# A tuned attention-and-feed-forward kernel: the order of its five queues is read from a table, and 185 operations go to VectorE

## The chip, the cores and the metric

The kernel runs on one core of one Trainium2 chip. The metric is device time in microseconds (us) of one execution, the median of the runs shown. A core has five instruction queues that matter here: TensorE (PE; its weight loads are listed apart as PEld), VectorE (DVE), ScalarE (ACT), GpSimd (POOL) and SyncE (SP), which in this kernel only issues DMAs. Each queue runs its own instructions in order, and the queues meet through semaphores.

## The reference

```python
def phi(x):                                   # q and k scaled by D ** -0.25
    h = x @ omega.T - sum(x * x, -1) / 2
    return exp(h - max(h, -1)) / sqrt(M)
kv, z = phi(k)^T @ v, sum(phi(k), tokens)     # one batch and head at a time
x = phi(q) @ kv / (phi(q) @ z + 1e-6)         # heads laid side by side: 4608 x 512
out = leaky_relu(x @ w_in, 0.01) @ w_out      # 512 -> 2048 -> 512
```

Eight batches of 576 tokens, eight heads of 64, 128 random features; everything in and out is float32.

## The kernel before, in words

**The work.** Attention goes batch by batch over the keys (`key_batch`) and in nine blocks of 512 tokens over the queries (`query_block`), two heads at a time. A float32 operand is written as two float16 parts (`high` copies the upper part, L479 on ACT or its twin L473 on DVE; `low_` subtracts to get the lower one, L485, on POOL or DVE), and a product is three float16 matmuls. For one unit of two heads (class `Unit`) the chain is: load (`nat`, L719), square on ACT (L722), sum on DVE (L724), scales (L729 to L734), split (L479 and L747 or L485), DMA transpose `t<-z` (L749), projection on PE (L762), maximum and subtraction on DVE (L770 to L790), exponential on ACT (L793), split again (L479, L485), and for queries two DMA transposes `qp<-ph` (L1060) and the product with the key sums on PE (L1092 to L1094). A finished block is turned by DMA into `xt` (L1029). The first two key batches and the first query block take a shorter way (class `Whole`, L846, L975, L1099).

**The feed-forward part.** For each block of 512 tokens PE runs a first layer (L1254 for blocks 0 and 1; L1308 from block 2 on, in a form that needs seven products in place of eight, whose weights `w<-w1d` are loaded for each product, L1298) and a second (L1490; L1415 for the last block, `TAIL`). These two are TensorE's filler between the attention pieces. One operation of the plan on PE is 6 matmuls of 512 columns or 12 of 256. Results leave PSUM by ACT or DVE (L479, L1324, L1263, L1331) and are split into `big` (L479, L485).

**The order.** Nothing is ordered by hand. Each operation is registered with `ways` (engine, modelled cost, function to call). `Plan.forward` (L195) lays all operations on five modelled queues one after another; for an operation with two ways it takes the engine that looks free first, weighted by `PRICE`. Its list is the program's order: `for o in plan.order(): o.run()` (L1548). The numbers of operations are the order in which the kernel registers them, so a number means the same operation before and after. Heat operations (L569) are matmuls without use that the planner puts into gaps of PE near the start. Constants steer the planner: `PACE`, `AFTER`, `SLACK`, `NUDGE`, `LATER`, `PRICE`, and the modelled landing of a DMA, `DMA`. 701 operations have a choice of engine; before, 700 of them are on ACT (548) or POOL (152) and one is on DVE.

Of the kernel before, what the change touches and what calls it, by code (L numbers as in the profile page):

```python
# [30 lines left out]
SIGN_POOL = {"w1": [0, 1, 2, 4, 5, 7], "w2": [0, 1, 3, 7]}  # L31
SPLIT_DVE = {"w1": [0, 1, 2, 4, 5, 7], "w2": [0, 1, 2, 3, 4, 5, 6]}
Z_POOL = {"k": 4, "q": 3}
PACE = {"k": 17.0506, "q": 9.3419, "w1": 0, "w1s": 4.2874, "w2": 12.4675, "w2s": 14.7789}

WHOLE = 2
FIRST_FAST = 2
TURNED = 1
HEAT = True
AFTER = {"w1": 0.0, "w1s": 0.0, "w2": 0.0, "w2s": 0.0, "k1": 0.0, "q1": 0}  # L40
PASSES = 0
SHIFT_OP = {180: -1.13, 6: -3.99, 178: 2.07, 213: -0.22, 420: 3.05, 572: -0.02, 480: -0.72, 242: -1.74, 250: -2.72, 106: -1.06, 268: -4.94, 148: -4.28, 85: -4.22, 813: 0.8, 510: 2.03, 109: 2.11, 452: 11.66, 574: 2.34, 243: -2.55, 245: -6.52, 430: 4.22, 69: 19.05, 135: 1.83, 476: -3.51, 209: -10.73, 167: 1.07, 75: -11.31, 536: -3.21, 54: 2.69, 203: -3.67, 218: -23.73, 152: 1.07, 137: -0.51, 238: -0.14, 168: 2.42, 811: 24.59, 116: -2.3, 454: -3.25, 518: -0.29, 44: 0.47, 494: -5.44, 239: -5.28, 580: 6.23, 191: -6.7, 855: 8.61, 275: -6.71, 236: 4.8}
WHOLE_ACT = ['k10']
EDGE_ACT = ['k02', 'k03']
SQ_POOL = ['k02', 'k13', 'q02']
LOW_ACT = {"w1": [3], "w2": [1, 4, 5]}
FFN_MI = [2, 2]
TAIL = 7
ROWS_LATE = 4
TAIL_ON = {"A11": ["DVE"], "A22": ["DVE"], "S1": ["POOL"], "S3": ["POOL"], "S2": ["DVE"], "A12": ["DVE"], "S4": ["POOL"], "T1": ["DVE"], "T2": ["DVE"], "T3": ["POOL"], "T4": ["DVE"]}  # L50
TAIL_DOWN = 2.0 ** -2
OPS = ("A11", "A12", "A22", "S1", "S2", "S3", "S4")
SLOT = {"B11": 0, "B21": 1, "B22": 2, "B12": 3, "T1": 4, "T3": 5, "T2": 6, "T4": 7}
SLACK = {"PE": 0.5, "t": 0.5608, "qp": 0, "ph": 0.6854, "mx": 0, "w": 0.2511, "chain": 0}
# [30 lines left out]

class Op:
# [3 lines left out]
class Plan:  # L90
# [21 lines left out]
    def op(self, ways, r=(), w=(), prio=0.0, slack=0.0, moved=0):  # L112
# [235 lines left out]
def act(n, pointers=0):  # L348
    return 0.17 + n / 1195 + 0.06 * pointers
# [19 lines left out]
def performer_ffn(ctx: ExitStack, tc, qT, kT, qn, kn, vn, omT, eye, w_in, w_out, out):  # L369
# [143 lines left out]
    def power_of_two(mx, name, prio, one_=ONE):  # L513
# [60 lines left out]
    class Weight:  # L574
# [27 lines left out]
        def convert(self, i, prio):  # L602
# [22 lines left out]
            def sums():  # L625
# [76 lines left out]
    class Unit:  # L702
# [49 lines left out]
        def features(self, c0, nc_, ph, part):  # L752
# [54 lines left out]
    class Whole:  # L807
# [5 lines left out]
        def __init__(self, what, i, hp, prio):  # L813
# [20 lines left out]
        def features(self, c0, nt, p32, p):  # L834
# [5 lines left out]
            def project():  # L840
# [101 lines left out]
    def key_batch(b, prio):  # L942

        plan.group = f"v{b}"
        plan.after = AFTER["k1"] if b == 1 else 0.0
        values(b, prio)
# [4 lines left out]
        for hp in range(HP):  # L951
            plan.like("k", PACE["k"])
            plan.after = AFTER["k1"] if b == 1 else 0.0
            plan.group = f"k{b}{hp}"
# [13 lines left out]
            if b < WHOLE:  # L968
                def sums(u=u, edge=edge, acc=acc, hp=hp, parts=parts):
# [232 lines left out]
    def tail_weights():  # L1202

        for q in range(4):
# [20 lines left out]
            for name, i in (("T3", 2), ("T2", 1), ("T1", 0), ("T4", 3)):  # L1225
# [3 lines left out]
                low_(512, lambda part=part: part(1), lambda t=t, i=i: t(i), lambda part=part: part(0),  # L1229
                     engines=TAIL_ON[name], r=[key(i), (tt, 0)], w=[(tt, 1)], prio=LATER["t"])  # L1230

    def feed_forward(j):
# [38 lines left out]
        def split(name, q, g):  # L1271
# [325 lines left out]
```

## Time and profile before

| | us |
|---|---|
| median of 3 runs | 926.81 (924.36 to 930.95) |
| the profiled execution's own time | 923.68 |
| its span, first to last instruction | 921.9 |
| PE busy in the span | 892.6 (97%) |
| DVE busy | 734.2 (80%) |
| ACT busy | 604.0 (66%) |
| POOL busy | 347.5 (38%) |
| DMA, share of 16 engines, mean | 74% |

Busy is the time in which an engine has at least one instruction under way. Matmuls overlap and their ends are modelled, so a PE that is busy 97% of the time is read together with its list of waits. The span is 1.8 us under the execution's own time.

### The profile page before, as it was taken

The page shows a single profiled execution, that of the slowest core. Times are in us where ns is not written, and L with a number is a line of the kernel's source. Part 1 is how long each engine was busy: PE and PEld are TensorE (multiplying, and loading weights), DVE is VectorE, ACT ScalarE, POOL GpSimd, SP SyncE. Part 2 cuts the span into 40 slices and gives each one's busy share as a digit, 9 for nine tenths or more (in the row PEclk, how much of TensorE's full clock was granted, in tenths as well). Part 3 has the DMA queues.
Part 4 walks back from the last instruction along what each step waited for, and adds up shares of the span by engine and source line. Part 5 has one row for each costly group of instructions (what it writes and reads, how often), then busy time and mean ns, then how long its engine had stood idle before and what let it go on. Part 6 is the DMA issues. An engine that isn't in the chain of part 4 may idle for free.

```text
span 921.9 us, 20740 instructions
## 1 busy us (share of the span) xinstructions
PE 892.6 (97%) x8247; PEld 641.4 (70%) x8247; DVE 734.2 (80%) x1390; ACT 604.0 (66%) x945; POOL 347.5 (38%) x297
## 2 busy tenths in 40 slices
PE   7999999999989999999999989999999999999998
PEld 6887554555547875687558855785579656888887
DVE  6998988887878989777787888889789789862751
ACT  6787896577655975388558864796568645842741
POOL 2422567579532560136013611261124622330330
PEclk9999999999999999999999999999999999999999
DMA  9976547855599998989689988897679963733401
GB/s 352 366 241 183 116 107 190 187 111 124 125 255 240 279 226 182 198 231 227 155 174 249 249 178 197 208 259 170 153 191 259 199 137 113 198 75 94 135 2 47
DMA packets 274881, 170.14 MB, mean 185 GB/s; under 512 B 191072, under 2 KB 237920, under 8 KB 273760
## 3 DMA queue, kind: packets, MB, share of 16 engines
q1 hardware_dynamic: 274784, 168.82, 73.9%
q8 instruction: 64, 1.05, 0.5%
q14 instruction: 33, 0.27, 0.1%
HBM read 105.87 MB, written 16.78 MB: 133 GB/s over the span
## 4 chain that ended last, share of the span: by engine, by line
PE 67%; DVE 14%; DMA 9%; ACT 5%; issue 3%; SPq 2%; POOL 1%; DVEq 0%; ACTq 0%; POOLq 0%
PE ffn L1490 11%; PE late L1490 10%; PE late L1308 10%; PE ffn L1308 9%; DMA t<-z 6%; PE late L1415 5%; PE ffn L1254 4%; PE pj L762 4%; PE late L1254 4%; PE ffn L1415 3%; DMA qp<-ph 2%; PE mi L975 2%; DVE ph L485 1%; DVE st L770 1%; DVE p L790 1%
## 5 line engine op out<-in xcount | busy, mean ns | idle before, releaser
L1308 PEld LDWEIGHTS <-w 128*128 128x128 f16 x2352 | 228.4, 98 | 34.8 <-issue 5.1
L485 POOL TENSOR_TENSOR big<-row,big 128x512 f16<-128x512 f32 x118 | 155.6, 1331 | 199.8 <-ACT big L479 183.7
L1490 PEld LDWEIGHTS <-big 128*128 128x128 f16 x1344 | 128.5, 98 | 140.6
L1490 PE MATMUL ffn<-wt,big 128*128 128x512 f16 x672 | 156.3, 379 | 0.0
L1490 PE MATMUL late<-wt,big 128*128 128x512 f16 x672 | 156.1, 379 | 0.0
L1308 PE MATMUL late<-xt,w 128*128 128x256 f16 x864 | 118.0, 273 | 0.7 <-ACT nat L479 0.7
L1308 PE MATMUL ffn<-xt,w 128*128 128x256 f16 x840 | 115.6, 273 | 1.0 <-ACT row L479 1.0
L793 ACT ACTIVATE p<-p,little 128x1024 f32<-128x1024 f32 (+1 forms) x60 | 61.0, 1017 | 65.5 <-DVE p L790 61.2
L770 DVE TENSOR_REDUCE st<-pj 128x8 f32<-128x1024 f32 x68 | 73.3, 1077 | 26.0 <-PE pj L762 25.9
L479 ACT ACTIVATE big<-row 128x512 f16<-128x512 f32 x130 | 78.8, 625 | 4.1 <-DVE row L1280 3.4
L485 DVE TENSOR_TENSOR ph<-p,ph 128x1024 f16<-128x1024 f32 x56 | 72.5, 1294 | 5.6 <-ACT ph L479 5.6
L762 PEld LDWEIGHTS <-t 128*128 128x128 f16 x944 | 57.2, 98 | 16.4 <-DMA t<-z 5.8
L762 PE MATMUL pj<-om,t 128*128 128x128 f16 x944 | 63.9, 219 | 4.1 <-DMA t<-z 2.7
L790 DVE SCALAR_TENSOR_TENSOR p<-pj,sc,st 128x1024 f32<-128x1024 f32 (+1 forms) x60 | 67.1, 1118 | 0.9
L724 DVE TENSOR_REDUCE sq<-z 128x8 f32<-128x512 f32 (+1 forms) x56 | 39.6, 708 | 32.9 <-ACT z L722 32.6
L1254 PEld LDWEIGHTS <-w 128*128 128x128 f16 x384 | 36.7, 98 | 40.4
L722 ACT ACTIVATE z<-nat 128x512 f32<-128x512 f32 (+1 forms) x56 | 36.4, 653 | 35.7 <-DMA t<-z 31.9
L479 ACT ACTIVATE ph<-p 128x1024 f16<-128x1024 f32 x56 | 59.1, 1055 | 0.9
L1308 PE MATMUL late<-w,w 128*128 128x256 f16 x324 | 53.0, 272 | 2.1 <-ACT row L479 2.1
L485 POOL TENSOR_TENSOR xn<-xp,xn 128x768 f16<-128x768 f32 (+1 forms) x16 | 27.7, 1733 | 69.0 <-ACT xn L479 68.2
L1308 PE MATMUL ffn<-w,w 128*128 128x256 f16 x324 | 53.0, 273 | 0.0
L1331 ACT ACTIVATE row<-row 128x512 f32<-128x512 f32 x72 | 44.5, 625 | 7.8 <-DVE row L1324 7.6
(272 smaller groups left out, 1847.3 us busy)
## 6 DMA issues: line engine op xcount, KB each, us to landing
w<-w1d SPq DMA_DIRECT2D x196, 256.0 KB, 3.4
v<-vn SPq DMA_DIRECT2D x28, 650.0 KB, 4.8
big<-w_in SPq DMA_DIRECT2D x8, 1024.0 KB, 11.7
big<-w_out SPq DMA_DIRECT2D x8, 1024.0 KB, 5.9
nat<-qn SPq DMA_DIRECT2D x32, 256.0 KB, 3.6
out<-row SPq DMA_DIRECT2D x29, 256.0 KB, 2.5
w1d<-wt SPq DMA_DIRECT2D x16, 256.0 KB, 3.1
nat<-kn SPq DMA_DIRECT2D x12, 320.0 KB, 4.2
```

The costliest lines, as they stand in the source:

```text
L479: ("ACT", act(n, int(pointer)), lambda: nc.scalar.activation(dst(), src(), AF.Copy, scale=1.0 if scale is None else value()), False),
L485: return ways([(e, c, lambda g=g: g.tensor_tensor(dst(), a(), b(), op=ALU.subtract), True) for e, c, g in (("POOL", pool_(n), nc.gpsimd), ...
L724: op("DVE", dve(n), lambda: nc.vector.tensor_reduce(at(self.sq)[:, :2 * nt], square().rearrange("p (g d) -> p g d", d=D), axis=AX.X, op=AL ...
L762: nc.tensor.matmul(at(pj)[:, 512 * h + c * M:512 * h + (c + 1) * M], at(self.t)[:, 2 * (c0 + c) + h, :], om[:, w, :], start=(w == 0), stop ...
L770: op("DVE", dve(n * M), lambda: nc.vector.tensor_reduce(row(0), pv(), axis=AX.X, op=ALU.max), r=[pj], w=[st], prio=prio)
L790: op("DVE", dve(n * M), lambda: nc.vector.scalar_tensor_tensor(p(), pv(), down(), row(2).rearrange("p (g o) -> p g o", o=1).broadcast_to([ ...
L793: op("ACT", act(n * M, 1), lambda: nc.scalar.activation(flat(p()), flat(p()), AF.Exp, bias=shift), w=[p32], r=["ones"], prio=prio)
L1254: nc.tensor.matmul(at(ph), wk[wp][:, c:c + P], xt[:, 512 * xp:512 * xp + 512], start=(i == 0), stop=(i == 3 * KT - 1))
L1308: nc.tensor.matmul(pair(bank)[:, f], wt[:, k, wp, f * P:f * P + P], operand(xname, k, xp), start=(first and f == k == i == 0), stop=(k == ...
L1331: op("ACT", act(512), lambda: nc.scalar.activation(at(g), at(src), AF.Prelu, scale=H_DOWN * (TAIL_DOWN if tail else 1.0), alpha=0.01), r=[ ...
L1415: nc.tensor.matmul(pair(bank)[:, t], g()[:, gp, f, t * P:t * P + P], operand(wname, 2 * q + f, wp), start=(first and q == t == f == i == 0 ...
L1490: nc.tensor.matmul(at(po), g_(q)[:, s, gp, t * P:(t + 1) * P], wf[wp], start=(q == s == 0 and gp == wp), stop=(q == s == 3 and gp == 1))
```

## The change

`Plan.order` still calls the planner, with other constants, and buffers get their places from it. Then, since the table `ORDER` is not empty, 185 operations listed in `ON` are set to DVE and the planner's list is replaced by the table's. The tiles, the loops, the buffers' numbers and the arithmetic are the same.

```diff
-AFTER = {"w1": 0.0, "w1s": 0.0, "w2": 0.0, "w2s": 0.0, "k1": 0.0, "q1": 0}
+AFTER = {"w1": 0.0, "w1s": 0, "w2": 0, "w2s": 0.0, "k1": 13.2731, "q1": 0}
-SQ_POOL = ['k02', 'k13', 'q02']
-LOW_ACT = {"w1": [3], "w2": [1, 4, 5]}
+SQ_POOL = ['k13', 'q02']
+LOW_ACT = {"w1": [0, 3], "w2": [1, 2, 4, 5]}
-TAIL_ON = {"A11": ["DVE"], ... "T3": ["POOL"], "T4": ["DVE"]}
+TAIL_ON = {"A11": ["POOL"], ... "T3": ["DVE"], "T4": ["DVE"]}
-DMA = {"turn": 0.9497, "land": 1.9}
+DMA = {"turn": 0.959, "land": 1.9}
-PRICE = {"PE": 1.0, "ACT": 0.5, "DVE": 27.4627, "POOL": 1.0, "SP": 1.0}
+PRICE = {"PE": 1.0, "ACT": 0, "DVE": 27.4627, "POOL": 1.0804, "SP": 1.0}
...
+ORDER = [
+    2, 0, 16, 1, 144, 151, 27, 3, 165, 43, 17, 4, 62, 22, 9, 5, 7, 18, 6, 145, 23, 146, 152, 3478, 19, 81, 3461, 158,
...
+    2092, 1879, 1869, 1894, 2300, 1880, 2091, 1886, 2340, 2071, 2319, 2289, 1887, 2288, 2075, 2361, 2301, 2128, 2072,
+    1888, 2341, 2302, 2342, 1895, 2343, 2303, 2306, 2093, 2320, 2304, 1912, 2094, 2290, 1902, 2151, 2307, 2658, 2076,
...
+]
+ON = {
+    102: "DVE", 282: "DVE", 309: "DVE", 310: "DVE", 340: "DVE", 360: "DVE", 365: "DVE", 369: "DVE", 375: "DVE",
...
+}
...
             done = self.forward()
+        if ORDER:
+            by = {o.number: o for o in done}
+            assert len(by) == len(ORDER)
+            for n, e in ON.items():
+                o = by[n]
+                o.engine, (o.cost, o.run, o.held) = e, o.ways[e]
+            done = [by[n] for n in ORDER]
         return done
```

`PACE`, `SLACK`, `NUDGE` and `LATER` change too. Read operation by operation, with the numbers of the kernel before:

- **Engines.** Of the 185 operations in `ON`, 131 were on ACT and 54 on POOL. The POOL ones are 41 splits of `big`, 11 of `xn`, 2 of `wt` (all L485). Of the ACT ones 98 copy from SBUF (55 of them a `row` into `big` or its last-block twin `g7`, 512 elements each) and 33 from PSUM. 154 of the 185 stand between 80 and 800 us of the trace before, 30 behind 800, one before 80.
- **Order.** PE's operations keep 168 of 768 places; the mean shift is 1.8 places and the largest 14. The mean shift is 2.3 places on ACT, 3.1 on DVE, 1.1 on POOL and 4.6 on SP.
- **Distance between a DMA and its first user**, counted as the PE work that the list has between the two (1.31 us for a PE operation of the feed-forward part, by its duration in the trace):

| DMA | list before, median | table, median | under 4 us, before / table | under 5.2 us, before / table |
|---|---|---|---|---|
| `qp<-ph`, L1060, 64 | 5.5 | 6.5 | 20 / 2 | 28 / 10 |
| `t<-z`, L749, 56 | 5.3 | 6.5 | 7 / 4 | 18 / 13 |
| `w<-w1d`, L1298, 196 | 17.8 | 14.9 | 0 / 3 | 0 / 8 |

Inside a run of seven products (L1308), an operation that adds to a bank after ScalarE has copied it out stands 1.31 us of PE work or more behind the operation that filled the bank before, and 2.6 us or more in the table. The shortest distance of a weight load is 11.8 us before; in the table the eight shortest are 3.6, 3.9, 3.9, 4.3, 4.4, 4.8, 4.8 and 4.8 us. As an example, transpose 2092 (`qp<-ph`) and its user 2093 have the PE operations 1887, 1895, 1888 between them before (3.9 us) and 1894, 1886, 1887, 1888, 1895, 2306 in the table (6.7 us).

- **Start.** Ahead of the first feed-forward operation (296, L1254) the list before has 54 operations of PE and 89 of DVE; the table has 56 and 91. The 1024 KB load of the first weight piece (144) is issued as the fourth DMA that moves data, before as the seventh.

## Rows read from the trace of the kernel before

**Rows 1.** Windows: us, then each engine's busy time, clock, DMA share, GB/s
```profile
0.00:80.00 80.00, 69.14 (x798) 63.14 (x799) 69.63 (x123) 58.73 (x80) 25.95 (x20) 0.98 0.86 308
80.00:800.00 720.00, 705.59 (x6373) 472.88 (x6373) 608.07 (x1185) 494.08 (x770) 294.71 (x257) 1.00 0.81 189
800.00:922.00 122.00, 117.88 (x1080) 105.41 (x1078) 56.54 (x83) 51.18 (x97) 26.81 (x21) 0.99 0.27 77
```

**Rows 2.** Waits of PE, 80 to 800 us: total us, times, longest
```profile
PE mi L1094 <- DMA qp<-ph: 6.0, 7, 2.1
PE pj L762 <- DMA t<-z: 2.7, 5, 1.3
PE late L1308 <- ACT row L479: 2.1, 2, 1.4
PE pj L762 <- DVE p L790: 1.4, 3, 0.6
PE ffn L1308 <- ACT row L479: 1.0, 2, 0.7
PE late L1308 <- ACT nat L479: 0.7, 1, 0.7
PE mi L1092 <- DMA qp<-ph: 0.3, 1, 0.3
```

**Rows 3.** Timeline of PE: start us, us, what, idle before and its releaser
```profile
546.41 0.20 PE L1093 MATMUL mi<-kv,qp 128*128 128x65 f16 x1
548.68 0.20 PE L1094 MATMUL mi<-kv,qp 128*128 128x65 f16 x1 [2.08 <-DMA qp<-ph]
```

**Rows 4.** Line L1060, the transposes of queries
```profile
L1060 SPq DMA_TRANSPOSE qp<-ph x64: 1231/1252/3188, 116.0 to 754.6; - x64
...
DMA to landing us min/median/max: 3.0/3.5/7.3
```

**Rows 5.** Line L749, the transposes ahead of the projection
```profile
L749 SPq DMA_TRANSPOSE t<-z x56: 1231/1304/2842, 99.3 to 738.2; - x56
...
DMA to landing us min/median/max: 3.0/4.0/7.4
```

**Rows 6.** Line L1298, the weight loads of the first layer
```profile
DMA to landing us min/median/max: 2.5/3.4/6.4
```

**Rows 7.** Groups: line, engine, tiles, count; busy us, mean ns; idle before
```profile
L485 POOL TENSOR_TENSOR big<-row,big 128x512 f16<-128x512 f32 x118 | 155.6, 1331 | 199.8 <-ACT big L479 183.7 <-PE ffn L1308 14.5 <-DVE st L780 1.3
L479 ACT ACTIVATE big<-row 128x512 f16<-128x512 f32 x130 | 78.8, 625 | 4.1 <-DVE row L1280 3.4
L1324 DVE TENSOR_TENSOR row<-ffn,row 128x512 f32<-128x512 f32 x40 | 27.3, 685 | 8.9 <-ACT row L479 4.6 <-PE ffn L1308 4.1
L780 DVE SCALAR_TENSOR_TENSOR st<-st,sc,sq 128x8 f32<-128x8 f32 (+1 forms) x60 | 23.6, 393 | 0.3
```

**Rows 8.** Single lines on DVE: ns min/median/max, first and last start
```profile
L485 DVE TENSOR_TENSOR big<-row,big x12: 679/692/1282, 795.6 to 890.5; 128x512 f16<-128x512 f32 x12
```

**Rows 9.** The same for L619, a DVE operation with one SBUF input
```profile
L619 DVE TENSOR_SCALAR wt<-wt x12: 680/683/1593, 11.7 to 103.3; 128x1024 uint32<-128x1024 uint32 x12
```

**Rows 10.** The same for L780, an 8-element DVE operation with SBUF inputs
```profile
L780 DVE SCALAR_TENSOR_TENSOR st<-st,sc,sq x60: 191/220/1349, 109.1 to 746.7; 128x8 f32<-128x8 f32 x48, 128x2 f32<-128x2 f32 x12
```

**Rows 11.** Timeline of DVE, 235 to 239 us
```profile
236.36 1.22 DVE L485 TENSOR_TENSOR z<-nat,z 128x512 f16<-128x512 f32 x1
237.50 1.12 DVE L780 SCALAR_TENSOR_TENSOR st<-st,sc,sq 128x8 f32<-128x8 f32 x1
238.65 2.06 DVE L781 SCALAR_TENSOR_TENSOR st<-sq,st 128x8 f32<-128x8 f32 x1
```

**Rows 12.** Timeline of POOL in the same stretch
```profile
237.41 1.19 POOL L485 TENSOR_TENSOR big<-row,big 128x512 f16<-128x512 f32 x1 [0.38 <-ACT big L479]
238.56 2.13 POOL L485 TENSOR_TENSOR wt<-wt,wt 128x1024 f16<-128x1024 f32 x1
```

**Rows 13.** Chain that ended last, in order of time: start, us, what
```profile
410.75 1.31 PE late L1308 x12
```

More of the change, by code (lines that the diff above doesn't have):

```diff
@@ L33 @@
 Z_POOL = {"k": 4, "q": 3}
-PACE = {"k": 17.0506, "q": 9.3419, "w1": 0, "w1s": 4.2874, "w2": 12.4675, "w2s": 14.7789}
+PACE = {"k": 17.0506, "q": 9.3419, "w1": 0, "w1s": 4.0808, "w2": 12.256, "w2s": 14.7789}
 WHOLE = 2
@@ L49 @@
 ROWS_LATE = 4
-TAIL_ON = {"A11": ["DVE"], "A22": ["DVE"], "S1": ["POOL"], "S3": ["POOL"], "S2": ["DVE"], "A12": ["DVE"], "S4": ["POOL"], "T1": ["DVE"], "T2": ["DVE"], "T3": ["POOL"], "T4": ["DVE"]}
+TAIL_ON = {"A11": ["POOL"], "A22": ["DVE"], "S1": ["POOL"], "S3": ["POOL"], "S2": ["DVE"], "A12": ["DVE"], "S4": ["POOL"], "T1": ["DVE"], "T2": ["DVE"], "T3": ["DVE"], "T4": ["DVE"]}
 TAIL_DOWN = 2.0 ** -2
@@ L53 @@
 SLOT = {"B11": 0, "B21": 1, "B22": 2, "B12": 3, "T1": 4, "T3": 5, "T2": 6, "T4": 7}
-SLACK = {"PE": 0.5, "t": 0.5608, "qp": 0, "ph": 0.6854, "mx": 0, "w": 0.2511, "chain": 0}
-NUDGE = {"k00": -25.85, "w24": 1.48, "q61": -21.35, "k10": 1.26, "k51": 12.31, "q00": -3.82, "k53": 5.68, "w20": -28.23, "w2s6": 9.28, "k12": -43.23, "w1s0": 20.35, "q41": 14.5, "w1s4": -31.95, "w2s5": 11.73, "q72": -10.0, "q03": -13.54, "w1s7": 11.67, "w2s7": 35.19, "k61": -6.69, "w13": -6.9, "w2s3": -4.27, "q10": 7.76, "s1": 15.36, "k50": -31.99, "q70": 16.75, "q02": -0.99, "q40": 0.78, "k42": 7.0, "w25": 5.84, "q63": -12.37, "w27": 17.73, "k11": -8.86, "w26": -23.6, "w2s2": -6.21, "v0": 2.9, "s4": 26.82, "k20": -6.57, "w2s1": -14.47, "q13": 74.22, "w2s4": 0.58, "s5": -0.19, "k02": -14.86, "q32": -6.67, "k62": -10.59, "w14": -8.71, "q11": -1.54, "q01": -26.27, "q62": 19.06, "w1s1": 23.47, "q22": -11.17, "v1": 56.53, "q20": -2.28, "w21": 0.21, "q81": -4.21, "k32": -5.66, "w22": 5.41, "q42": -23.84, "w16": 25.18, "q80": 26.73, "k01": -35.93, "v7": -21.02, "q83": 11.84, "s0": -8.64, "k71": 9.99, "q71": -17.15, "w2s0": -2.21, "w23": 2.17, "w1": 3.97, "q60": 18.36, "q53": -3.85, "v4": 9.32}
@@ L56 @@
-DMA = {"turn": 0.9497, "land": 1.9}
+SLACK = {"PE": 0.5, "t": 0.5608, "qp": 0, "ph": 0.7205, "mx": 0.3817, "w": 0.2686, "chain": 0}
+NUDGE = {"k00": -34.58, "w24": 0.31, "q61": -21.35, "k10": 1.26, "k51": 18.64, "q00": -9.35, "k53": 5.68, "w20": -27.85, "w2s6": 11.07, "k12": -43.23, "w1s0": 20.05, "q41": 14.5, "w1s4": -34.51, "w2s5": 11.73, "q72": -10.0, "q03": -13.54, "w1s7": 3.85, "w2s7": 35.19, "k61": -6.69, "w13": -6.72, "w2s3": -4.27, "q10": 7.76, "s1": 15.36, "k50": -31.99, "q70": 16.75, "q02": -0.99, "q40": 0.78, "k42": 7.0, "w25": 5.84, "q63": -12.37, "w27": 14.68, "k11": -8.86, "w26": -75.24, "w2s2": 14.2, "v0": 2.9, "s4": 26.82, "k20": -6.57, "w2s1": -14.47, "q13": 78.87, "w2s4": 25.02, "s5": -18.23, "k02": -14.86, "q32": -3.42, "k62": -7.66, "w14": -30.08, "q11": -1.54, "q01": -26.27, "q62": 19.06, "w1s1": 23.47, "q22": -11.17, "v1": 47.01, "q20": -2.28, "w21": 21.39, "q81": -4.21, "k32": -5.66, "w22": 19.42, "q42": -23.84, "w16": 25.18, "q80": 26.73, "k01": -35.93, "v7": -28.3, "q83": 11.84, "s0": -8.64, "k71": 18.32, "q71": -17.15, "w2s0": -2.21, "w23": -4.68, "w1": 3.97, "q60": 18.36, "q53": -3.28, "v4": 10.69, "w11": -66.92, "q73": 5.16, "k33": -16.25, "w1s3": 13.51, "w1s2": -13.38, "q23": -12.35, "k03": -0.78, "w12": 12.32, "s6": 10.1, "q12": 3.31, "k31": 5.31, "w15": 2.14, "w2": -2.65, "k70": -10.63, "s7": -2.01}
@@ L60 @@
 SUMS_DVE = [2, 6]
-LATER = {"w1": -37.7982, "w2": 48.514, "k": -26.2825, "q": -902.8399, "t": 0.05, "f": 0.0319, "s": -0.0449}
+LATER = {"w1": -37.7982, "w2": 48.514, "k": -17.5267, "q": -866.6901, "t": 0.0594, "f": 0.0319, "s": -0.0696}
 ONE = 2.0 ** 14
@@ L83, in __init__ @@
         self.kind, self.place, self.ops, self.left, self.last = kind, None, [], 0, None
+ORDER = [
[172 rows of a table added]
+]
+ON = {
+    102: "DVE", 282: "DVE", 309: "DVE", 310: "DVE", 340: "DVE", 360: "DVE", 365: "DVE", 369: "DVE", 375: "DVE",
+    415: "DVE", 483: "DVE", 534: "DVE", 561: "DVE", 596: "DVE", 607: "DVE", 632: "DVE", 667: "DVE", 685: "DVE",
+    690: "DVE", 695: "DVE", 700: "DVE", 704: "DVE", 705: "DVE", 715: "DVE", 720: "DVE", 725: "DVE", 730: "DVE",
+    735: "DVE", 745: "DVE", 813: "DVE", 828: "DVE", 851: "DVE", 861: "DVE", 908: "DVE", 953: "DVE", 956: "DVE",
+    963: "DVE", 1040: "DVE", 1088: "DVE", 1096: "DVE", 1104: "DVE", 1134: "DVE", 1140: "DVE", 1170: "DVE",
+    1203: "DVE", 1259: "DVE", 1278: "DVE", 1281: "DVE", 1288: "DVE", 1297: "DVE", 1316: "DVE", 1322: "DVE",
+    1365: "DVE", 1366: "DVE", 1373: "DVE", 1378: "DVE", 1390: "DVE", 1391: "DVE", 1398: "DVE", 1399: "DVE",
+    1404: "DVE", 1411: "DVE", 1419: "DVE", 1422: "DVE", 1430: "DVE", 1443: "DVE", 1462: "DVE", 1468: "DVE",
+    1508: "DVE", 1528: "DVE", 1538: "DVE", 1590: "DVE", 1600: "DVE", 1651: "DVE", 1688: "DVE", 1695: "DVE",
+    1704: "DVE", 1712: "DVE", 1748: "DVE", 1787: "DVE", 1792: "DVE", 1804: "DVE", 1813: "DVE", 1819: "DVE",
+    1850: "DVE", 1865: "DVE", 1868: "DVE", 1874: "DVE", 1910: "DVE", 1982: "DVE", 2004: "DVE", 2026: "DVE",
+    2034: "DVE", 2041: "DVE", 2052: "DVE", 2118: "DVE", 2127: "DVE", 2140: "DVE", 2141: "DVE", 2146: "DVE",
+    2147: "DVE", 2158: "DVE", 2173: "DVE", 2178: "DVE", 2179: "DVE", 2191: "DVE", 2198: "DVE", 2199: "DVE",
+    2205: "DVE", 2227: "DVE", 2244: "DVE", 2274: "DVE", 2372: "DVE", 2385: "DVE", 2409: "DVE", 2416: "DVE",
+    2434: "DVE", 2440: "DVE", 2471: "DVE", 2483: "DVE", 2496: "DVE", 2497: "DVE", 2528: "DVE", 2529: "DVE",
+    2532: "DVE", 2537: "DVE", 2540: "DVE", 2541: "DVE", 2549: "DVE", 2554: "DVE", 2572: "DVE", 2581: "DVE",
+    2604: "DVE", 2609: "DVE", 2610: "DVE", 2615: "DVE", 2616: "DVE", 2704: "DVE", 2740: "DVE", 2753: "DVE",
+    2777: "DVE", 2788: "DVE", 2838: "DVE", 2841: "DVE", 2855: "DVE", 2905: "DVE", 2926: "DVE", 2935: "DVE",
+    2980: "DVE", 2995: "DVE", 3002: "DVE", 3025: "DVE", 3031: "DVE", 3040: "DVE", 3049: "DVE", 3052: "DVE",
+    3061: "DVE", 3064: "DVE", 3080: "DVE", 3100: "DVE", 3162: "DVE", 3165: "DVE", 3166: "DVE", 3216: "DVE",
+    3219: "DVE", 3240: "DVE", 3244: "DVE", 3249: "DVE", 3252: "DVE", 3267: "DVE", 3282: "DVE", 3286: "DVE",
+    3294: "DVE", 3309: "DVE", 3312: "DVE", 3321: "DVE", 3333: "DVE", 3336: "DVE", 3339: "DVE", 3345: "DVE",
+    3363: "DVE", 3378: "DVE", 3394: "DVE", 3414: "DVE", 3415: "DVE",
+}
```

169 rows, old and new, of the table ORDER are left out of this document.

## The prediction, made before the changed kernel ran

> **What bounds the kernel now.** I read the windows first, then the waits of TensorE (PE), then single lines. In the windows [rows 1] the reader is to see three stretches. From 80 to 800 us PE is busy 705.59 of 720 us, so 14.4 us are idle. In the first 80 us it idles 10.9 us while VectorE (DVE) is busy 69.63 of 80, its densest stretch (87%): the start is paced by DVE. Behind 800 us PE is busy 117.88 of 122 us and the other engines are under half busy; the rest is mostly the end, when the last result is stored. So PE is the bound, its arithmetic is untouched, and only its idle time can be won.
>
> The waits between 80 and 800 us [rows 2] sum to 14.2 us: 9.0 us for transposes (6.0 + 2.7 + 0.3, 13 waits), 3.8 us for ScalarE (ACT) copying a bank out (2.1 + 1.0 + 0.7, five waits), 1.4 us for DVE. One of them shows what such a wait is: PE had begun a product, and its second half of `qp` came 2.08 us late [rows 3].
>
> **The change, part by part.**
>
> *Transposes issued farther ahead.* A `qp` transpose lands 3.0 us after its issue at best, 3.5 in the median and 7.3 at worst [rows 4]; `t` takes 3.0, 4.0 and 7.4 [rows 5]. The list before has 27 of the 120 less than 4 us of PE work ahead of their user; the table has 6. Nearly every late one is moved by one PE operation, 1.31 us [rows 13]; the one of rows 3 goes from 3.9 to 6.7 us, more than its wait. The gain lies between 0 (the issue itself slips, since a transpose leaves only when its split is done) and 9.0 us. I scale the wait by the count of short distances, 6 of 27, which leaves 2.0 us: **-7.0 us**. I lean to this end because the longest wait, 2.1 us, is under two operations.
>
> *Bank copies.* Each of the five waits for ACT is at most 1.4 us, and the table puts one more operation of 1.31 us between such a pair. Between 0 and -3.8 us; I take **-3.0 us**, since ACT also gets shorter: 131 operations at about 0.63 us [rows 7] leave it, some 82 of its 604 us. The 1.4 us that wait for DVE I leave as they are.
>
> *Weight loads issued later.* This is what the table pays with. Eight of 196 loads now stand less than 5.2 us ahead of their product and three less than 4 us, against 11.8 us or more before; they land in 2.5 us at best, 3.4 in the median, 6.4 at worst [rows 6]. At the median nothing is late. If all eight landed at the worst time (distances 3.6, 3.9, 3.9, 4.3, 4.4, 4.8, 4.8, 4.8 us) they would cost 2.8 + 2.5 + 2.5 + 2.1 + 2.0 + 3 x 1.6 = 16.7 us. So 0 to +16.7; nearest to the median, **+1.0 us**.
>
> *185 operations to DVE.* Their price there:
> - 54 from GpSimd (POOL), 32256 elements per partition. The same split on DVE takes 692 ns for 512 [rows 8], against 1331 ns on POOL [rows 7]: 43.6 us.
> - 33 from PSUM, at 685 ns for 512 [rows 7]: 20.2 us.
> - 98 copies from SBUF, 58112 elements. DVE does no such copy in the trace. Nearest is L619, one SBUF input, 683 ns for 1024 [rows 9]: 38.8 us. The other end is the two-input split's pace, 692 for 512: 78.5 us. I take the lower, since L619 has the same number of inputs.
>
> Of this 88.7 us (low) or 121.3 us (high) fall between 80 and 800, where DVE has 608.07 us busy and 112 us idle [rows 1]. Neighbours on DVE overlap by 0.08 us (236.36 + 1.22 against 237.50) [rows 11], so 154 more instructions give back 12 us. That makes 685 us (95%) or 717 us (99.6%), before what POOL's lighter load gives back. L780 works on 8 elements in 220 ns but took up to 1349 [rows 10]: it started at 237.50 beside a POOL split of 237.41 to 238.60 and ended with it, and the next, at 238.65, lasted as long as POOL's 2.13 us [rows 11, 12]. So DVE loses time to POOL, and POOL loses 54 operations, about 81 of its 347 us. L780's waits alone are 60 x (393 - 220) ns by its mean [rows 7], 10 us; I put the whole relief at 5 to 20 us by that one line, and nothing of it in the sum. What covers the added DVE work is the distances above; if that cover is gone, each step of a unit's chain passes its delay to the next transpose. Cost at the low price: **0**, at the high price the rival below.
>
> The Trainium skill, "SBUF — State Buffer", section "Who interferes with whom", speaks against part of this: VectorE and GpSimd share a port pair, a copy in a two-port mode takes it for its whole length, "PE and ACT never wait on anyone". The trace agrees on the lock (220 to 1349 ns, above). By that rule the 98 copies, free of waits on ACT, enter the contention; the sum would then lose the relief and nothing more, since the 54 splits leave it.
>
> *Smaller edits.* Two weight conversions get their first step on ACT in place of DVE, one square goes from POOL to ACT, four splits of the last block go from DVE to POOL and four the other way. All have free time beside them in the first or last stretch: 0, at most 1 us either way.
>
> *Start and end.* PE's and DVE's work ahead of the first feed-forward operation grows by two operations each, at most +3 us; the first weight piece is loaded earlier, into a DVE that idles 10 us, at most -5 us. I take 0. The end keeps its order of stores: 0.
>
> *Queues passed.* SP issues in order and waits in order. A transpose that moves ahead is moved past plain loads; a load that waits for its ring place then holds the transposes behind it. That is inside the bounds of the first and third part.
>
> **Sum**: -7.0 - 3.0 + 1.0 = -9.0 us on the profiled execution's 923.7, so 914.7. The median of the runs stands 3.1 us above that execution, which was the lowest. What separates the runs is not shown; I keep a little of it and forecast **915 us**.
>
> **The rivals.**
> - *DVE takes over what the DMAs gave.* The transposes are issued late because their splits are: DVE at 95% runs each unit's chain later by about what the table gained. For: DVE is the fullest engine off the bound, and the operation at 238.65 shows how late a small step on it can be [rows 11]. Against: POOL's relief. Gain of the first part gone, ACT's kept: 923.7 - 3 + 1 = 922, with the median's excess **924 us**.
> - *Weight loads late (slower).* Place: the runs of products between 290 and 875 us. Price: 16.7 us, and the transposes queued behind gain nothing: 923.7 + 16.7 - 3.0 = 937. It decides from the point at which these loads land later than 4.4 us on the average. **937 us.** Against: the median of 3.4.
> - *DVE at the high price (slower).* At 99.6% with no relief it must run without any idle time; its densest stretch reached 87%. If 95% is the most it can do, 717 us need 755: **about 958 us**. Against: L619's pace.
> - *More than the sum.* All 14.2 us of waits go and the start gives 4: **905 us**.
> - *The table does not say what I read*: the chip's order would be the same but for the engines; then about 926 us. The replay is plain in the diff, so this is small.
>
> **How the numbers follow.** About 1% (9.3 us) is what a measurement of this kernel can tell from no change. Chances: forecast 0.55 (its own range 909 to 921, two thirds of it under 917.5), DVE takes over 0.20, more than the sum 0.12, weight loads 0.07, DVE at the high price 0.04, the rest 0.02. Faster: 0.37 + 0.12 + 0.02 = 0.51; same: 0.18 + 0.18 + 0.02 = 0.38; slower 0.11. The range goes from 904 to 930: below it lies little of the fourth case, above it the two slow ones.
>
> **What would show it.** Right: PE's waits for `qp` and `t` between 80 and 800 us fall from 9.0 to about 2 us, those for ACT from 3.8 to under 1, PE idle there from 14.4 to some 6 us; DVE's busy time in that stretch rises to between 660 and 700 us and L780's mean falls from 393 ns. Wrong: a new wait of PE for `w<-w1d`; copies on DVE at 0.6 us or more for 512 elements; waits for DVE above 5 us; or a start whose first feed-forward matmul comes more than 3 us later than before.

## The result and the profile after

| us | before | after |
|---|---|---|
| median | 925.59 (923.56 to 930.95, 4 runs) | 916.88 (916.53 to 917.65, 4 runs) |
| profiled execution, own time | 923.68 | 917.65 |
| its span | 921.9 | 915.9 |

The ratio of the medians is 0.9898, with a 95% interval of 0.9854 to 0.9942: about 1% faster, 1.9 us above the forecast. The profiled executions differ by 6.0 us, the medians by 8.7 us.

Line numbers of the changed kernel are about 208 higher (L485 is L693, L780 is L988, L1060 is L1268, L1308 is L1516, L762 is L970). The windows of the changed kernel answer to [rows 1]: stretch, then busy time of PE, PEld, DVE, ACT and POOL, clock, DMA share, GB/s.

```profile
0.00:80.00 80.00, 68.53 (x787) 63.82 (x788) 69.42 (x119) 59.02 (x78) 20.26 (x19) 0.96 0.76 273
80.00:800.00 720.00, 710.11 (x6443) 478.44 (x6443) 670.95 (x1347) 440.69 (x678) 207.71 (x204) 1.00 0.81 193
...
sum 960.00, PE 889.41 PEld 641.11 DVE 804.44 ACT 530.65 POOL 260.28; mean PE 296.47 PEld 213.70 DVE 268.15 ACT 176.88 POOL 86.76
```

Between 80 and 800 us PE's idle time fell from 14.4 to 9.9 us while DVE's busy time went from 608 to 671 us. PE's waits in that stretch, which answer to [rows 2] (total us, times, longest; the first line is the last of the view before, which those rows leave out, the others are those after):

```profile
PE mi L519 <- DVE little L904: 0.2, 1, 0.2
...
PE pj L970 <- DVE p L998: 6.2, 6, 2.6
PE pj L970 <- DMA t<-z: 1.5, 1, 1.5
PE mi L1300 <- DVE xp L1324: 0.8, 2, 0.5
PE late L1516 <- ACT row L687: 0.7, 1, 0.7
PE mi L1300 <- DVE kv L1223: 0.3, 1, 0.3
PE ffn L1248 <- DVE xp L1324: 0.2, 1, 0.2
```

The change of kind matters more than the total. Transposes: 9.0 to 1.5 us. ScalarE: 3.8 to 0.7 us. VectorE: 1.6 to 7.5 us (1.4 + 0.2 before; 6.2 + 0.8 + 0.3 + 0.2 after). So -7.5 - 3.1 + 5.9 = -4.7 us, against a fall in idle time of 4.5 us; gaps too short for the list make up the rest. A wait for a weight load stands in neither list.

The rest of the span's 6.0 us: PE idles 0.6 us more in the first 80 us and 1.1 us more behind 800 us (115.9 - 110.77 against 121.9 - 117.88), and its busy time is 3.2 us shorter. Of that, 1.8 us are heat matmuls: 127 with 15.5 us before (L569), now this group (mean ns of one behind the busy time):

```profile
L777 PE MATMUL mi<-om 128*128 128x240 f16 x119 | 13.7, 268 | 1.0 <-DVE r L1320 1.0
```

-4.5 + 0.6 + 1.1 - 3.2 = -6.0. The remaining 1.4 us of busy time I could not place; ends of matmuls are modelled.

Single lines of the changed kernel (ns min/median/max; then issue to landing in us), which answer to [rows 4 to 6], [rows 10] and the unknown price of a copy on DVE:

```profile
L1268 SPq DMA_TRANSPOSE qp<-ph x64: 1231/1251/3286, 124.8 to 748.6; - x64
...
DMA to landing us min/median/max: 3.0/3.5/6.2
...
L1506 SPq DMA_DIRECT2D w<-w1d x196: 319/432/2182, 245.7 to 860.3; - x196
...
DMA to landing us min/median/max: 2.5/3.7/6.4
...
L988 DVE SCALAR_TENSOR_TENSOR st<-st,sc,sq x60: 191/220/1719, 110.0 to 741.8; 128x8 f32<-128x8 f32 x48, 128x2 f32<-128x2 f32 x12
...
L683 DVE CAST big<-row x39: 411/420/1376, 101.6 to 889.5; 128x512 f16<-128x512 f32 x39
...
L683 DVE CAST ph<-p x10: 680/694/697, 328.1 to 663.2; 128x1024 f16<-128x1024 f32 x10
...
L683 DVE COPY row<-late x6: 677/681/691, 316.6 to 872.1; 128x512 f32<-128x512 f32 x6
```

Transposes land in the median as before (`qp` 3.5 us; `t` 3.9 against 4.0 us); their users stand farther off. A copy of 512 elements from SBUF costs DVE 0.420 us, between the two ends of the prediction (0.34 and 0.69) and near the low one; from PSUM 0.681 us, as assumed. The groups that answer to [rows 7] (busy us, mean ns):

```profile
L693 POOL TENSOR_TENSOR big<-row,big 128x512 f16<-128x512 f32 x81 | 99.3, 1235 | 255.1 <-ACT big L687 163.3 <-DVE big L683 70.5 <-ACT z L930 7.7
L988 DVE SCALAR_TENSOR_TENSOR st<-st,sc,sq 128x8 f32<-128x8 f32 (+1 forms) x60 | 16.2, 270 | 0.5
```

The 8-element line fell from 393 to 270 ns on the mean with its median still 220: fewer of its instructions run into one of POOL's. Counted singly in the timelines, 16 of the 60 took over 0.35 us before and 6 after, and every one of them stood beside a POOL instruction.

### The profile page after: what moved, and what is told of

The parts are those of the page before. It is cut to its first block, busy times and chain, and to the rows that moved or that the text cites. A ratio compares the mean times of both kernels' runs of the same rounds, so it can differ in the third digit from the quotient of the medians.

```text
span 915.9 us, 20523 instructions
## 1 busy us (share of the span) xinstructions
PE 889.4 (97%) x8239; PEld 641.1 (70%) x8239; DVE 804.4 (88%) x1573; ACT 530.7 (58%) x813; POOL 260.3 (28%) x246
## 3 DMA queue, kind: packets, MB, share of 16 engines
q8 instruction: 64, 1.05, 0.5%
## 4 chain that ended last, share of the span: by engine, by line
PE 66%; DVE 24%; DMA 4%; issue 3%; ACT 2%; SPq 0%; DVEq 0%; ACTq 0%
PE late L1516 12%; PE ffn L1516 11%; PE late L1698 10%; PE ffn L1698 10%; PE ffn L1623 4%; PE pj L970 4%; PE late L1623 3%; PE ffn L1462 3%; PE late L1462 3%; DVE ph L693 2%; DVE st L978 2%; DVE p L998 2%; DMA t<-z 2%; DVE st L1070 1%; DVE sq L932 1%
## 5 line engine op out<-in xcount | busy, mean ns | idle before, releaser
L1516 PEld LDWEIGHTS <-w 128*128 128x128 f16 x2352 | 228.0, 98 | 31.7 <-issue 2.0
L693 POOL TENSOR_TENSOR big<-row,big 128x512 f16<-128x512 f32 x81 | 99.3, 1235 | 255.1 <-ACT big L687 163.3
L1516 PE MATMUL late<-xt,w 128*128 128x256 f16 x918 | 125.2, 273 | 0.6 <-DVE nat L1647 0.6
L1516 PE MATMUL ffn<-xt,w 128*128 128x256 f16 x786 | 108.2, 273 | 0.0
L693 DVE TENSOR_TENSOR ph<-p,ph 128x1024 f16<-128x1024 f32 x56 | 71.7, 1280 | 4.2 <-ACT ph L687 4.0
L970 PE MATMUL pj<-om,t 128*128 128x128 f16 x944 | 63.8, 219 | 7.8 <-DVE p L998 6.2
L970 PEld LDWEIGHTS <-t 128*128 128x128 f16 x944 | 57.5, 98 | 17.5 <-issue 8.1
L998 DVE SCALAR_TENSOR_TENSOR p<-pj,sc,st 128x1024 f32<-128x1024 f32 (+1 forms) x60 | 67.2, 1119 | 1.0
L687 ACT ACTIVATE big<-row 128x512 f16<-128x512 f32 x90 | 54.8, 625 | 4.0 <-DVE row L1488 3.3
L1516 PE MATMUL late<-w,w 128*128 128x256 f16 x330 | 54.0, 273 | 0.8 <-ACT row L687 0.7
L1516 PE MATMUL ffn<-w,w 128*128 128x256 f16 x318 | 52.1, 273 | 0.0
L1462 PE MATMUL ffn<-xt,w 128*128 128x512 f16 x216 | 50.2, 379 | 0.0
L687 ACT ACTIVATE ph<-p 128x1024 f16<-128x1024 f32 x46 | 48.4, 1052 | 0.7
L693 POOL TENSOR_TENSOR v<-xp,v 128x1024 f16<-128x1024 f32 (+1 forms) x11 | 24.3, 2207 | 80.9 <-ACT v L687 71.4
```

What stands on the lines that cost most here:

```text
L687: ("ACT", act(n, int(pointer)), lambda: nc.scalar.activation(dst(), src(), AF.Copy, scale=1.0 if scale is None else value()), False),
L693: return ways([(e, c, lambda g=g: g.tensor_tensor(dst(), a(), b(), op=ALU.subtract), True) for e, c, g in (("POOL", pool_(n), nc.gpsimd), ...
L998: op("DVE", dve(n * M), lambda: nc.vector.scalar_tensor_tensor(p(), pv(), down(), row(2).rearrange("p (g o) -> p g o", o=1).broadcast_to([ ...
L1462: nc.tensor.matmul(at(ph), wk[wp][:, c:c + P], xt[:, 512 * xp:512 * xp + 512], start=(i == 0), stop=(i == 3 * KT - 1))
L1516: nc.tensor.matmul(pair(bank)[:, f], wt[:, k, wp, f * P:f * P + P], operand(xname, k, xp), start=(first and f == k == i == 0), stop=(k == ...
```

## Experiments

Each ratio below is against the kernel before, timed beside the variant; its median there was 926.6 to 928.4 us. The changed kernel itself was timed beside a kernel before of 925.59 us, so a difference between a variant and the changed kernel is given as the difference of the medians and can be off by some 2 to 4 us, which the ratios' intervals leave open. Where an experiment edits the table, one of its shifts stands for all.

**The table's order without the engine moves.** The two parts of the change are taken apart; first the order alone.

```diff
-ON = {
-    102: "DVE", 282: "DVE", 309: "DVE", ...
-}
+ON = {}
```

> The table's order with the list of 185 engine moves left empty: those operations stand at the same places of the list but on ScalarE and GpSimd. Theory 'distance' (the gain comes from transposes issued farther ahead of their users): 917 to 920 us, DMA waits of PE between 80 and 800 us at 1 to 3 us. Rival 'engines' (the gain comes from taking work off ScalarE and GpSimd): 924 us or more, with new waits for ScalarE and GpSimd.

934.20 us, ratio 1.0075 (1.0049 to 1.0102): slower than before, and 17 us above the changed kernel. The first row is the windows' middle stretch, then PE's longest waits there and DVE's (in this kernel L946 is the projection, L974 the DVE operation that releases `pj`, the one PSUM tile of the projections, "the bank" below, and L663 ACT's copy):

```profile
80.00:800.00 720.00, 694.62 (x6264) 461.43 (x6265) 609.68 (x1169) 483.40 (x756) 272.20 (x252) 1.00 0.79 189
...
PE pj L946 <- DVE p L974: 14.3, 17, 2.6
PE late L1492 <- ACT row L663: 3.9, 4, 2.0
...
PE ffn L1492 <- ACT row L663: 1.7, 3, 1.1
...
DVE ph L669 <- ACT ph L663: 26.1, 19, 3.2
```

No wait for a transpose is in the list: the distances do to these waits what was read from them, yet the time is on the side of 'engines'. PE idles 25.4 us here, 14.4 before. Its waits for ACT's bank copies are 5.6 us (3.9 + 1.7), 3.8 before, though the users stand farther off. And DVE, with 61 us less to do than in the changed kernel, stands 26.1 us behind ACT's copies of `ph`, against 4.0 us there and 5.6 us before; PE waits 14.3 us for the bank, which DVE frees later in the same queue.

**The engine moves without the table.** The same 185 operations go to DVE, in the order of the list before.

```diff
             done = self.forward()
+        by = {o.number: o for o in done}
+        for n, e in ON.items():
+            o = by[n]
+            o.engine, (o.cost, o.run, o.held) = e, o.ways[e]
         return done
```

> The kernel before with its own list, and only the 185 operations set to VectorE. 'Distance': nothing is won, DMA waits of PE stay near 9 us, and waits for VectorE come on top: 925 to 930 us. 'Engines': 917 to 920 us.

955.75 us, ratio 1.0311 (1.0284 to 1.0339). PE's waits, 80 to 800 us:

```profile
PE pj L770 <- DVE p L798: 5.5, 4, 2.9
PE pj L770 <- DMA t<-z: 5.1, 5, 2.5
PE mi L1102 <- DMA qp<-ph: 4.5, 4, 2.3
PE late L1316 <- ACT row L487: 4.3, 5, 1.1
PE ffn L1316 <- ACT row L487: 3.9, 4, 1.8
PE mi L1100 <- DVE kv L1017: 3.2, 1, 3.2
```

Both expectations are missed by 25 us or more. Waits for transposes stay at 9.6 us (`t` up from 2.7 to 5.1, `qp` down from 6.3 to 4.5), waits for ACT grow from 3.8 to 8.7 us and waits for DVE from 1.6 to 17.0 us (the two shown and four smaller lines). Neither the order nor the whole set of moves is faster by itself.

**The moves by their source.** With the table's order, the 131 operations taken from ACT alone, then the 54 taken from POOL alone.

```diff
-ON = {102: "DVE", 282: "DVE", 309: "DVE", 310: "DVE", 340: "DVE", ...}
+ON = {102: "DVE", 282: "DVE", 309: "DVE", 369: "DVE", 415: "DVE", ...}
```

> The changed kernel with the 131 moves from ScalarE kept and the 54 from GpSimd taken back. Theory 'chain' (a unit's steps wait for ScalarE's queue in turn, so the ScalarE moves are what the table lives on): VectorE's waits for ScalarE in the splits stay low and the time is 918 to 923 us. Rival 'port' (what counts is GpSimd's load, which holds VectorE up): 926 us or more, with VectorE's small operation L988 slow again.

```diff
-ON = {102: "DVE", 282: "DVE", 309: "DVE", 310: "DVE", 340: "DVE", ...}
+ON = {310: "DVE", 340: "DVE", 360: "DVE", 365: "DVE", 375: "DVE", ...}
```

> The changed kernel with the 54 moves from GpSimd kept and the 131 from ScalarE taken back. 'Chain': VectorE waits 20 us or more for ScalarE's splits of ph and PE waits 10 us or more for VectorE's L998; 928 to 935 us. 'Port': 918 to 922 us.

ACT's moves alone: 928.18 us, 0.9998 (0.9980 to 1.0016). POOL's alone: 922.25 us, 0.9940 (0.9919 to 0.9961). With the table's order and

| moved | neither | ACT's 131 | POOL's 54 | both |
|---|---|---|---|---|
| median, us | 934.20 | 928.18 | 922.25 | 916.88 |
| ratio to before | 1.0075 | 0.9998 | 0.9940 | 0.9898 |

By the medians ACT's moves give 5 to 6 us and POOL's 11 to 12; by the ratios, which carry the spread of the kernel before, 4 to 7 and 9 to 13. Both times are on the side of 'port': 928.18 us where 926 or more was expected, 922.25 us where 918 to 922 was. The signs of 'chain' did not come either: with ACT's copies back, DVE's wait for `ph` was 17.5 us, not 20, and PE's for the bank 5.7 us, not 10. The last column's interval overlaps that of POOL's moves alone (0.9854 to 0.9942 against 0.9919 to 0.9961), but its runs lie 4 us below that kernel's lowest, 921.62. The windows and waits of ACT's moves alone:

```profile
80.00:800.00 720.00, 702.24 (x6328) 470.45 (x6329) 648.93 (x1277) 432.85 (x665) 280.40 (x255) 1.00 0.80 191
...
PE pj L946 <- DVE p L974: 11.8, 9, 2.6
...
DVE ph L669 <- ACT ph L663: 9.2, 8, 2.5
```

and of POOL's alone:

```profile
80.00:800.00 720.00, 708.87 (x6393) 475.39 (x6392) 628.87 (x1241) 493.57 (x773) 203.21 (x203) 1.00 0.80 191
...
PE pj L946 <- DVE p L974: 5.7, 7, 2.2
...
DVE ph L669 <- ACT ph L663: 17.5, 17, 3.2
```

Moving ACT's copies cuts DVE's wait for `ph` (26.1 to 9.2 us) but the bank stays late (14.3 to 11.8 us); moving POOL's splits leaves more of the wait for `ph` and frees the bank sooner (5.7 us). PE's idle time in the stretch is 25.4 us with neither, 17.8 with ACT's moves, 11.1 with POOL's and 9.9 with both. On top of POOL's moves, then, ACT's take 1.2 us of it and none from the bank (5.7 and 6.2 us); of the 4.5 us between these two spans 2.4 are shorter busy time of PE, so by which wait they act there is not shown.

The 8-element line's mean, 423 ns with neither, is 348 with ACT's moves and 332 ns with POOL's; 20, 12 and 13 of its 60 instructions took over 0.35 us, each beside a POOL instruction. It falls as far with ACT's moves, though POOL's busy time over the span is then no shorter (338 against 331 us). So it does not measure POOL's load alone, as I used it, but which instructions meet.

**The new constants with no table.**

```diff
-ORDER = [
-    2, 0, 16, 1, 144, ...
-]
+ORDER = []
```

`ON` stays in the file, but it is read only where `ORDER` is not empty.

> The changed kernel's planner constants with an empty table: neither the order nor the engines of the table. If the constants carry the gain: 917 to 920 us. If the table does: 923 to 932 us, with waits for transposes as before.

927.59 us, 1.0014 (0.9989 to 1.0039): the constants alone, and with them the smaller edits, give nothing that these runs can tell from zero. PE's first waits are those of before, 7.3 us for `qp<-ph` and 3.8 us for `t<-z`.

**Distance taken away from the changed kernel.** Users of transposes go ahead of the feed-forward operation before them on PE: 120 of 132 users at once, then only those of `qp` (55), then only projections (65).

```diff
-... 266, 792, 316, 492, 512, 265, 468, 421 ...
+... 266, 792, 468, 316, 492, 512, 265, 421 ...
```

> The changed kernel, but 120 of the 132 PE operations that use a transpose are put ahead of the feed-forward operation that stands before them, so the distance shrinks by about 1.3 us again. 'Distance': DMA waits of PE return to 5 to 9 us and the time to 920 to 924 us. 'Engines': 917 us, as the changed kernel.

> The changed kernel with only the users of the query transposes (55 of 64 operations, L1300) put ahead of the feed-forward operation before them. Theory 'distance': PE's waits for qp, 0 in the changed kernel, come back to 3 to 6 us, time 920 to 923 us. Rival 'pj': the distance of these matters little, what the first shift lost was the projection's bank; then no waits for qp over 1 us and 917 to 918 us.

> The changed kernel with only the projections (65 of 68, L970) put ahead of the feed-forward operation before them. 'Pj' (one PSUM tile takes all projections, and VectorE must have read the one before): waits of PE for VectorE's L998 of 20 us or more, time 938 to 946 us, DMA waits under 3 us. 'Distance': waits for the transposes t of 4 us or more, 921 to 925 us.

All users: 947.47 us, 1.0211 (1.0184 to 1.0238). Users of `qp`: 920.79 us, 0.9934 (0.9910 to 0.9958). Projections: 951.85 us, 1.0269 (1.0238 to 1.0299). PE's waits with the `qp` users earlier:

```profile
PE pj L970 <- DVE p L998: 6.3, 6, 2.7
PE mi L1300 <- DVE xp L1324: 2.8, 2, 1.8
PE mi L1300 <- DMA qp<-ph: 2.2, 2, 1.4
...
PE mi L1302 <- DMA qp<-ph: 0.4, 1, 0.4
```

and with the projections earlier:

```profile
PE pj L970 <- DVE p L998: 27.9, 21, 4.6
...
PE pj L970 <- DMA t<-z: 1.9, 2, 1.2
```

All users at once cost 31 us, which neither theory foresaw. One place less for `qp` brings 2.6 us of transpose waits back, with 2.0 us more for DVE's `xp`, and about 4 us of time (its runs, 919.28 to 921.49, lie above all of the changed kernel's, though the intervals overlap): distance acts on this wait as predicted. The projections pay 35 us for one place, more than 'pj' expected, and hardly any of it to their transpose (1.9 us against 1.5): they run into the bank `pj`, which DVE's L998 has not yet read.

Not all of the 35 us is waiting. Of the 34.4 us between the two spans, 23.7 are idle time of PE between 80 and 800 us and 10.6 are longer busy time (900.0 against 889.4 us). Part of that is the clock, as the longest wait shows (PE's timeline, then the windows before and behind the wait, with the granted clock third from the end):

```profile
295.28 1.86 PE L970 MATMUL pj<-om,t 128*128 128x128 f16 x16 [4.64 <-DVE p L998]
...
284.00:290.00 6.00, 6.00 (x29) 2.74 (x28) 5.89 (x4) 3.97 (x5) 4.73 (x3) 1.00 0.43 107
296.00:300.00 4.00, 4.00 (x26) 3.07 (x25) 2.86 (x4) 1.19 (x3) 0.00 (x0) 0.50 0.73 217
```

PE worked at 2.4 GHz (1.00), idled 4.64 us and then worked at 1.2 GHz (0.50): its 16 projection matmuls took 1.86 us, where such a group of 16 took 1.05 us in the changed kernel behind a wait of 2.58 us. Behind a wait of 3.83 us at 533 us the same was seen. The mean granted clock of the execution is 0.987, 0.996 in the changed kernel.

A projection stands between two things, its transpose and the release of its bank, and one PE operation of 1.31 us is more than the room that it has on the bank's side.

**Distance added to the kernel before.** Users go behind the feed-forward operation that follows: 105 of 132 users at once, then only those of `qp` (49).

```diff
-... 2343, 2289, 2288, 2390, 2093, 2303, 2096, 2290, 2306, 1889 ...
+... 2343, 2289, 2288, 2390, 2303, 2290, 2306, 1889, 2093, 2096 ...
```

> The kernel before, no engine moved, but 105 of the 132 PE operations that use a transpose are put behind the feed-forward operation that follows them, so the distance grows by about 1.3 us. 'Distance': DMA waits of PE fall from 9 to about 3 us and the time to 918 to 922 us. 'Engines': 925 us or slower, since what follows these operations comes later.

> The kernel before, no engine moved, with only the users of the query transposes (49 of 64) put behind the feed-forward operation that follows them. 'Distance': waits for qp fall from 6 to about 2 us and the time to 921 to 924 us. Rival 'chain': what these operations release comes 1.3 us later each time and the time is 927 us or more, though the waits for qp fall.

All: 948.10 us, 1.0221 (1.0194 to 1.0248). `qp` alone: 933.05 us, 1.0071 (1.0044 to 1.0097), with these waits of PE:

```profile
PE pj L946 <- DMA t<-z: 7.4, 5, 2.8
PE late L1492 <- ACT row L663: 2.9, 3, 1.4
...
PE mi L1278 <- DMA qp<-ph: 0.7, 3, 0.2
```

The wait for `qp` goes from 6.3 to 0.7 us as the distance says, and the kernel is slower by 0.7%. DVE now waits 20.4 us for L1278's result, 11.3 before; it runs its queue in order, so I read the longer waits for `t` (2.7 to 7.4 us) as splits, and with them transposes, that leave later; the steps between were not followed. That is the side of 'chain' and, for all users, of 'engines'. More distance by itself is not the lever.

**The bank freed first.** In the changed kernel L988, the operation behind it and L998 go 1 to 10 places ahead in DVE's queue at six places where PE waited for the bank; in the second kernel the load of the identity also stands ahead of operation 16 again, since PE waits 4.7 us for it at the start of the changed kernel.

```diff
-... 1195, 1212, 1009, 1256, 788, 1194, 1196, ... 780, 1224, 1225, 1014 ...
+... 1195, 1224, 1212, 1009, 1256, 788, 1194, 1225, 1196, ... 780, 1014 ...
```

> The changed kernel; in the six places where PE waited for the projections' bank, VectorE's L988 to L998, which free it, are put 1 to 10 places ahead in VectorE's queue. If these waits are on the path: they fall from 6.2 us to about 1 and the time to 912 to 914 us. If what is put back is as urgent: 917 us, with other waits in their place.

```diff
-    2, 0, 16, 1, 144, 151,
+    2, 0, 1, 16, 144, 151,
```

> The kernel before this one (bank freed first), and the 64 KB load of ident put ahead of the first 320 KB load again, as in the kernel before the change. PE's first matmul starts 1.1 us earlier. If the start is set by that: 1 us less than the kernel with the bank freed first. If it is set by VectorE's work: the same.

921.28 us, 0.9928 (0.9900 to 0.9957), and 920.74 us, 0.9924 (0.9896 to 0.9952). Waits of PE in the first of them:

```profile
PE late L1516 <- ACT row L687: 2.5, 2, 1.8
...
PE ffn L1698 <- ACT row L1539: 1.8, 1, 1.8
PE pj L970 <- DVE p L998: 1.4, 1, 1.4
```

The wait for the bank falls from 6.2 to 1.4 us and others take its place. Neither gets near the 912 to 914 us of the first theory, and neither is better than the changed kernel: their runs begin at 919.55 and its runs end at 917.65, though the intervals overlap, so that they are worse is not shown. With the identity loaded first PE's first matmul starts 1.3 us earlier (3.65 against 4.95 us), but the first feed-forward matmul 0.9 us later (82.6 against 81.7 us). The identity's wait does not set the start; the 0.5 us between the two medians are within the spread of their runs.

## Why the prediction was right, and where its reasons were not

**Transposes issued farther ahead, -7.0.** Measured -7.5 us of waits (9.0 to 1.5). The two tests with `qp` users, in either direction, move the wait for `qp` as the distance says. Right as a wait; but as a gain of time it needs the moves. With the order alone these waits are gone and the kernel is 0.75% slower, and with `qp` users later they fall by 5.6 us and it is 0.7% slower.

**Bank copies, -3.0.** Measured -3.1 us (3.8 to 0.7). The number was right, the first reason not: with the same added distance and no moves these waits rose to 5.6 us. With ACT's moves alone they are 2.2 us, with POOL's alone 2.4, with both 0.7. The distance alone did not take them away; with the moves they went.

**Weight loads, +1.0.** No wait for `w<-w1d`, though the landing's median rose from 3.4 to 3.7 us. Too high by 1.0; the rival of late loads did not occur.

**185 operations to DVE, 0.** The step that failed, in two ways. First its sign and its weight: I took the moves as a load that something hides, and put the gain in the order. Without the moves the same order is slower than before, and the moves are worth some 17 us in it, about two thirds of them from the 54 POOL operations. I had written down the relief, 5 to 20 us by L780, and kept it out of the sum, and I subtracted ACT's shorter queue only where PE waited for ACT directly. What they shorten by the lists is DVE's wait for ACT's copies of `ph` (26.1 to 4.0 us), PE's wait for the bank (14.3 to 6.2 us) and its waits for ACT's bank copies (5.6 to 0.7 us); that the first leads to the second is my reading of the queue, and the bank follows POOL's moves more than ACT's. Second, the cost was not 0: PE's waits for DVE rose from 1.6 to 7.5 us. That has nearly the size of the rival in which DVE takes over, 5.9 of its 7 us, but it stands at the bank and not at the transposes, and beside the gain, not in place of it. My sign that it would be wrong, waits for DVE above 5 us, did come, and PE's idle time in the middle stretch came to 9.9 us where the sign of being right asked for some 6.

The longest of these waits shows the place. L1133's line (ns min/median/max), then DVE's timeline (start us, us):

```profile
L1133 DVE SCALAR_TENSOR_TENSOR v<-v,little,v x12: 1521/1544/3229, 136.5 to 633.5; 128x1280 f16<-128x1280 f32 x12
...
282.10 3.23 DVE L1133 SCALAR_TENSOR_TENSOR v<-v,little,v 128x1280 f16<-128x1280 f32 x1
...
288.17 1.28 DVE L998 SCALAR_TENSOR_TENSOR p<-pj,sc,st 128x1024 f32<-128x1024 f32 x1
```

POOL's in the same stretch:

```profile
280.89 3.09 POOL L693 TENSOR_TENSOR v<-xp,v 128x1024 f16<-128x1024 f32 x1 [1.03 <-ACT v L687]
```

and PE's (in brackets the idle time before, and its releaser):

```profile
289.50 1.05 PE L970 MATMUL pj<-om,t 128*128 128x128 f16 x16 [2.58 <-DVE p L998]
```

L1133's median is 1.544 us; this one ran 3.23 us beside a POOL split, 1.7 us too long, and L998 stands behind it in the queue. Without those 1.7 us the wait of 2.58 us would, by my estimate, have been about 0.9.

**DVE's load.** 670.95 us against 685 (low price) and 717 (high); the sign asked for 660 to 700. Right: the 39 copies cost 0.42 us, and DVE's high price is refuted. The rise of 62.9 us is 14 under the 77 of the low price, though these copies cost more than the 0.34 us taken there; L988's line alone gave 7.4 us back (23.6 to 16.2), so the relief that was left out of the sum is real.

**Port pair.** The Trainium skill's "SBUF — State Buffer", section "Who interferes with whom", spoke against the moved copies. The trace agrees on the lock itself (1.54 to 3.23 us above; L988 up to 1.719 us). That the copies would use up the relief is not seen. Of the 39 copies into `big` only three stand beside a POOL instruction; the longest of these took 1.376 us, and each of the other 36 0.43 us at most. Nor did the 54 splits leave the contention, as the prediction has it: on DVE a 512-element split into `big` took 0.683 us in the median and up to 1.528, one of them 1.34 us beside a POOL split (at 106.8 us). POOL's split takes 1235 ns after against 1331 before, but most of that fall came with the order: 1242 ns with neither set of moves, 1252 with ACT's alone, copies included.

**Start and end, 0.** The first feed-forward matmul starts at 83.83 us, 81.63 before: 2.2 us later, inside the bound. PE's idle time by stretches of the trace (us):

| stretch | before | after |
|---|---|---|
| 80 to 300 us | 4.2 | 5.6 |
| 300 to 600 us | 8.4 | 1.8 |
| 600 to 800 us | 1.9 | 2.5 |

The gain is made between 300 and 600 us; before and behind it a little is lost.

**The sum against the median.** The two profiled executions differ by 6.0 us, not 9.0. The middle stretch gave 4.5 us less than the sum, mainly because DVE's 5.9 us were priced at 0; that is the mis-sized term. The first and last stretches idle 1.7 us more, priced at 0 too. Against that, PE's busy time was 3.2 us shorter, which the prediction does not have at all. So 4.5 + 1.7 - 3.2 = 3.0 us were missing; 0.3 us had been added, and the changed kernel's median lies 0.8 us under its profiled execution: 3.0 - 0.3 - 0.8 = 1.9 us, the miss. That it is so small is in part luck. The medians differ by more than the profiled executions, 8.7 us, since the kernel before was profiled in one of its quickest runs: its runs spread over 7.4 us (923.56 to 930.95), those of the changed one over 1.1 us. Why the kernel before spreads is not settled. Fewer waits for DMA landings would be a guess; the table's order alone has none for transposes and still spreads over 4.9 us (932.74 to 937.59).

**Still open.** Whether POOL's moves act by the split's shorter time on DVE (0.69 against 1.33 us) or by fewer meetings of DVE and POOL was not separated; the 8-element line cannot tell, since it falls as far with ACT's moves. Nor is it shown why the waits won by freeing the bank first come back as waits for ACT.

## What to carry to other kernels

When queues run in order, a wait that PE shows names the last link only: read the waits of the engine that feeds it (here DVE's 26.1 us for `ph`) before pricing a move of work at zero. A new order and a new division of the work among engines are one change; each half alone was slower than the kernel that they improved together. A consumer that also waits for a buffer has room on two sides, so count the distance to the release as well as to the arrival before shifting it.

## What was not expected of the hardware

A DVE instruction beside a POOL split took about twice its median: 3.23 us against 1.544 (L1133). A copy of 512 float32 elements into float16 took DVE 0.420 us, while one of 1024 took 0.694 us, so the cost is not in proportion to the elements. Two orders that differ by one place of PE per projection differed by 35 us on the same work, 10.6 of them in longer busy time: behind a wait of 4.64 us PE's granted clock was 0.50 from 296 to 300 us.
